# Converting float64 weight blocks one step ahead of their matmuls, in a fused attention and gating kernel

## The chip, the cores and the metric

The kernel runs on one core of a Trainium2 chip. The metric is the device time of one execution in microseconds (us), as the median of several runs.

## The reference

Four batches of 448 tokens go through causal attention with 12 heads, then two mixing layers. Inputs are float64 and the result is float32. Cut to what matters:

```python
attn = softmax_causal(q @ k.T / sqrt(64)) @ v                  # 4 x 12 x 448 x 64
x = attn.transpose(0, 2, 1, 3).reshape(4, 448, 768)
gate = sigmoid(causal_conv5(x, conv_w))                        # 5 taps, each channel alone
x = (gate * (x @ w_val)) @ w_out
theta = x @ w_theta
zr, zi = x * cos(theta), x * sin(theta)
u = x + einsum('ts,bsd->btd', w_tok_r, zr) + einsum('ts,bsd->btd', w_tok_i, zi)
out = u + maximum(u @ w_ch, 0)
```

The four dense weights, w_val, w_out, w_theta and w_ch, are 768 x 768 each.

## The kernel before

The program is written for five engines: TensorE (PE, matmuls), VectorE (DVE), ScalarE (ACT), GpSimd (POOL) and SyncE (SP, which issues the transfers). It interleaves two streams. One is attention, in `attn_iter` (L673), one head in five segments: scores, row maximum by DVE (L360), exp by ACT (L118), transposes of the probabilities (L379), the product with v (L402), and, per pair of heads, the reciprocal of the sums (L418), which goes to DRAM in small packets (`rows<-rec`, L425) and comes back broadcast (`rb<-rows`, L451) to scale the attention's result (`xf`, L462). The other is `dense(b)` (L552): six output blocks each of w_val, w_out, w_theta and w_ch for one batch, all in transposed form with 128 channels per block. While batch b's dense stream runs, the attention of batch b+1 is advanced between its steps by a rate table.

A weight block, numbered n = 0 to 23 for the first batch (0 to 5 w_val, 6 to 11 w_out, 12 to 17 w_theta, 18 to 23 w_ch), holds 768 x 128 weights in two halves g. A half, written here as 16.0 or 16.1, passes through four steps:

- `load_w` (L197 on, issue at L202): SP brings 384 KB of float64 words into a buffer of tag "wb" (8 buffers), named `cv_raw`.
- `stage_w` (L210): `to_f32` (L153) builds float32 bits from the two 32-bit words of each number: DVE at L156 and L159 into a PSUM buffer `ps_cv`, ACT at L162, DVE at L163 back into `cv_raw`.
- `split_w` (L214): the float32 block is split into a high part of fewer bits (POOL, L107) and the rest (POOL, L110, or DVE, L113, in the first halves of w_theta), into a second "wb" buffer `w_hl`. The float32 block (`plain`, L221, w_val and w_out) or the split one (`scratch`, L242, w_theta and w_ch) is stored in DRAM for the later batches.
- In `gemm` (L519), 18 matmuls (L532) for a block: three for each 128 of the 768 inputs, high by high, high by low, low by high.

`gemm(n)` works half by half, and ahead of the matmuls of half g of block n it asks for the later blocks' steps. In the kernel before these are, at L524 to L527, the split of block n+1, the conversion of n+2, the load of n+3 (and for later batches the fetch from DRAM of n+3). Blocks 0 and 1 are multiplied inside the attention of batch 0, and blocks 0 to 3 are converted there (the table `A_TILES`), in the kernel before as in the changed one. From the second batch on no block is converted; blocks come back from DRAM (L250).

In the w_theta part, `theta(e)` makes for each block a tile `z`: t = theta/2pi (L587), rounding (L588, L589), absolute value (L591, on DVE in this batch), sine and cosine on ACT (L600, L601), products with x (L602 on DVE, L603 on POOL). `ztr` (L613) transposes z on PE, `tok` (L627) multiplies by the token weights. ACT needs a table load (ACT_TABLE_LOAD) between exp and sine. In the w_ch part each block ends with L665 on DVE, and transposes (L654) and an output store (L659).

The framework orders each engine's instructions when the program is built, with a model of time and of the data each one needs; on the chip every engine then works strictly in that fixed order, the queue of SP too. So moving one call in `gemm` can shift the place of many instructions.

Of the kernel before, what the change touches and what calls it, by code (L numbers as in the profile page):

```python
# [33 lines left out]
AHEAD = 2  # L34
# [17 lines left out]
def kernel(  # L52
# [46 lines left out]
    def f32(ap):  # L99
        return ap.bitcast(F32)  # L100

    def psum(tag):
        at = "mm" if tag == "mm" else "at"
        return ps.tile([P, 512], F32, tag=at, name=f"ps_{tag}", bufs=2 if tag == "mm" else 6)

    def pool_hi(dst, src):
        nc.gpsimd.tensor_scalar(out=dst, in0=src, scalar1=1.0, scalar2=0.0, op0=ALU.mult, op1=ALU.add)  # L107
# [45 lines left out]
    def to_f32(dst, raw):  # L153
        hi, lo = raw[:, :, 1], raw[:, :, 0]
        low = psum("cv")[: raw.shape[0], : raw.shape[1]].bitcast(I32)
        nc.vector.tensor_scalar(  # L156
            out=low, in0=lo.bitcast(U32), scalar1=2.0**-29, scalar2=7.0, op0=ALU.mult, op1=ALU.min
        )
        nc.vector.scalar_tensor_tensor(  # L159
            out=low, in0=hi, scalar=-(2**31), in1=low, op0=ALU.bitwise_and, op1=ALU.bitwise_or  # L160
        )
        nc.scalar.activation(lo.bitcast(F32), hi.bitcast(F32), AF.Abs, scale=2.0**-112)  # L162
        nc.vector.scalar_tensor_tensor(  # L163
            out=dst.bitcast(I32), in0=lo, scalar=3, in1=low, op0=ALU.logical_shift_left, op1=ALU.bitwise_or
        )
# [28 lines left out]
    def words(t):  # L194
        return t.rearrange("p n two -> p (n two)")[:, 0:CV]

    def load_w(n, g):  # L197
        if n >= NW:
            return
        e = n % KC  # L200
        t = pool.tile([P, CV, 2], I32, tag="wb", name="cv_raw", bufs=8)
        nc.sync.dma_start(  # L202
            out=t.rearrange("p (c n) two -> p c (n two)", c=KH),
            in_=stages[n // KC][g * KH * P : (g + 1) * KH * P, 2 * e * P : 2 * (e + 1) * P].rearrange(
                "(c p) n -> p c n", p=P
            ),
        )
        bits[n, g] = t

    def stage_w(n, g):  # L210
        if n < NW:
            to_f32(words(bits[n, g]), bits[n, g])

    def split_w(n, g):  # L214
        if (n, g) not in bits:
            return
        flat = words(bits.pop((n, g))).bitcast(F32)
        t = flat.rearrange("p (c n) -> p c n", n=P)
        kept = n % NW // KC in PLAIN
        if B > 1 and kept and n < NW:  # L220
            nc.sync.dma_start(out=plain[n, g], in_=flat)  # L221
        store = B > 1 and (kept and B > 2 if n >= NW else not kept)
        if n < AHEAD:
            hi, lo = (
                pool.tile([P, S], F32R, tag=tag, name="w_ahead", bufs=12)[:, : KH * P].rearrange("p (c n) -> p c n", n=P)
                for tag in ("act_hi", "act_lo")
            )
        else:
            hl = pool.tile([P, 2, KH, P], F32R, tag="wb", name="w_hl", bufs=8)
            hi, lo = hl[:, 0], hl[:, 1]  # L230
        if n < NW:
            pool_hi(hi, t)
        else:
            nc.scalar.copy(hi, t)  # L234
        (dve_lo if n < NW and int(W_DVE[n // KC]) > g else pool_lo)(lo, t, hi)
        if store and n < AHEAD:
            for a, x in enumerate((hi, lo)):
                nc.sync.dma_start(
                    out=scratch[n, g][:, a * KH * P : (a + 1) * KH * P], in_=f32(x.rearrange("p c n -> p (c n)"))
                )  # L240
        elif store:
            nc.sync.dma_start(out=scratch[n % NW, g], in_=f32(hl.rearrange("p a c n -> p (a c n)")))  # L242
        splits[n, g] = (hi, lo)

    def fetch_w(n, g):
        if not NW <= n < NW * B:
            return
        if n < 2 * NW and n % NW // KC in PLAIN:
            t = pool.tile([P, CV, 2], I32, tag="wb", name="cv_raw", bufs=8)
            nc.sync.dma_start(out=words(t).bitcast(F32), in_=plain[n % NW, g])  # L250
            bits[n, g] = t
            return
        hl = pool.tile([P, 2, KH, P], F32R, tag="wb", name="w_hl", bufs=8)
        nc.sync.dma_start(out=f32(hl.rearrange("p a c n -> p (a c n)")), in_=scratch[n % NW, g])
        splits[n, g] = (hl[:, 0], hl[:, 1])
# [263 lines left out]
    def gemm(acts):  # L519
        n = wn[0]  # L520
        wn[0] += 1
        pt = psum("mm")
        for g in range(2):
            split_w(n + 1, g)  # L524
            stage_w(n + 2, g)
            load_w(n + 3, g)
            fetch_w(n + 3, g)  # L527
            whi, wlo = splits.pop((n, g))
            for kc in range(g * KH, (g + 1) * KH):
                xhi, xlo = acts[kc]  # L530
                for m, (a, x) in enumerate(((whi, xhi), (whi, xlo), (wlo, xhi))):
                    nc.tensor.matmul(  # L532
                        pt[:, :S], lhsT=a[:, kc % KH, :], rhs=x,
                        start=kc == 0 and m == 0, stop=kc == KC - 1 and m == 2,
                    )
            if g == 0:
                yield
        return pt
# [13 lines left out]
    def dense(b):  # L552
# [8 lines left out]
        for e in range(KC):  # L561
            if b == 0 and e < AHEAD:
                pt = ahead.pop(e)
                if YLD:
                    yield
            else:
                pt = yield from gemm(xs)
            hf = pool.tile([P, S], F32, tag="tmp", name="hf")
            hf_ins.append(
                nc.vector.scalar_tensor_tensor(  # L570
                    out=hf, in0=gates.pop((b, e)), scalar=1.0, in1=pt[:, :S], op0=ALU.add, op1=ALU.mult
                )
            )
            h_hl[e] = hl(hf, dve=H_LO[b])
            yield
        for e in range(KC):
            pt = yield from gemm(h_hl)
            x2f[e] = pool.tile([P, S], F32, tag="x2f", name="x2f", bufs=6)
            nc.scalar.activation(x2f[e], pt[:, :S], AF.Copy, scale=0.5)
            x2_hl[e] = hl(x2f[e], 0.5, pt[:, :S], dve=O_LO[b])  # L580
            yield

        def theta(e):
            pt = yield from gemm(x2_hl)
            z = pool.tile([P, 2, S], F32, tag="z", name="z", bufs=3)
            t, kk = z[:, 1, :], z[:, 0, :]
            nc.scalar.activation(t, pt[:, :S], AF.Copy, scale=INV_2PI)  # L587
            nc.vector.tensor_scalar(out=kk, in0=t, scalar1=ROUND, scalar2=ROUND, op0=ALU.add, op1=ALU.subtract)  # L588
            nc.vector.tensor_tensor(out=t, in0=t, in1=kk, op=ALU.subtract)  # L589
            if ABS_DVE[b]:  # L590
                nc.vector.tensor_scalar(  # L591
                    out=kk.bitcast(I32), in0=t.bitcast(I32), scalar1=0x7FFFFFFF, scalar2=None, op0=ALU.bitwise_and
                )
            else:
                nc.scalar.activation(kk, t, AF.Abs)
            zri[e] = z
            with ExitStack() as st:
                for ins in exps[-PIN:]:
                    st.enter_context(tc.issue_after(ins.ins))
                nc.scalar.activation(t, t, AF.Sin, scale=TWO_PI)  # L600
                nc.scalar.activation(kk, kk, AF.Sin, bias=halfpi, scale=-TWO_PI)  # L601
            nc.vector.tensor_tensor(out=kk, in0=kk, in1=x2f[e], op=ALU.mult)  # L602
            (nc.vector if Z_DVE[b] else nc.gpsimd).tensor_tensor(out=t, in0=t, in1=x2f[e], op=ALU.mult)  # L603
            yield
# [190 lines left out]
```

## Time and profile before

| | us |
|---|---|
| median of 3 runs (lowest, highest) | 778.81 (778.42, 780.77) |
| the profiled execution's own time | 784.47 |
| its span | 782.4 |
| PE busy | 714.7 (91% of the span) |
| DVE busy | 463.3 (59%) |
| ACT busy | 445.0 (57%) |
| POOL busy | 331.9 (42%) |

The span is the time from the first to the last instruction that the profiler saw. The mean granted clock of PE was 0.967 of full speed. The trace gives each instruction's start and length, and for idle time of an engine ahead of an instruction what released it. The dense stream of batch 0, which alone converts blocks in `gemm`, runs from about 100 to 300 us.

### The profile page before, as it was taken

How to read it: one execution, taken by the hardware profiler on the slowest of the kernel's cores; microseconds unless marked ns; L12 is line 12 of the kernel's file. 1: busy time of each engine (PE TensorE's matmuls, PEld its weight loads, DVE VectorE, ACT ScalarE, POOL GpSimd, SP SyncE). 2: the span in 40 equal slices, each digit the busy share in tenths (PEclk: the TensorE clock that was granted, in tenths of full speed). 3: DMA queues.
4: the chain of work that ended last, by engine and by line, in shares of the span. 5: the costliest groups of instructions: out<-in, count | busy, mean ns of one | idle time of the engine just before them, and what ended most of it. 6: DMA issues, size and time to landing. Idle time of an engine off the chain costs nothing.

```text
span 782.4 us, 12216 instructions
## 1 busy us (share of the span) xinstructions
PE 714.7 (91%) x4009; PEld 607.5 (78%) x4009; DVE 463.3 (59%) x1104; ACT 445.0 (57%) x1047; POOL 331.9 (42%) x363
## 2 busy tenths in 40 slices
PE   5898978994988998999899999999899998999997
PEld 4665666783867886888688798898788887898996
DVE  4888599887777564463575564564576432115531
ACT  4787665876797454565877344354878331125401
POOL 0597774975476566774164410033062241201100
PEclk9999889998999999899999999999999999999999
DMA  9845337988684398799843288688532187774223
GB/s 227 181 122 146 78 106 224 208 265 187 193 143 123 103 208 279 233 224 338 152 75 99 54 171 232 193 141 240 143 61 66 52 135 233 203 220 139 84 71 81
DMA packets 152940, 125.78 MB, mean 161 GB/s; under 512 B 92815, under 2 KB 130477, under 8 KB 152877
## 3 DMA queue, kind: packets, MB, share of 16 engines
q1 hardware_dynamic: 152877, 125.00, 62.9%
q8 instruction: 32, 0.52, 0.3%
q14 instruction: 31, 0.25, 0.1%
HBM read 95.81 MB, written 29.16 MB: 160 GB/s over the span
## 4 chain that ended last, share of the span: by engine, by line
PE 58%; DVE 15%; ACT 10%; DMA 9%; issue 4%; POOL 2%; SPq 2%; DVEq 0%; ACTq 0%; POOLq 0%
PE ps_mm L532 31%; PE ps_mm L627 11%; PE ps_av L402 5%; PE ps_tr L379 3%; ACT prob L118 2%; DMA cv_raw<-in_moe_w_theta_dram 2%; PE ps_s L358 2%; PE ps_s L359 2%; DVE qs L113 2%; DMA scratch<-w_hl 2%; DVE ps_s L360 2%; DVE gate L494 2%; DVE klo L113 1%; DMA out_dram<-o 1%; DVE ps_cv L156 1%
## 5 line engine op out<-in xcount | busy, mean ns | idle before, releaser
L532 PE MATMUL ps_mm<-act_hi,w_hl 128*128 128x448 f32 x864 | 267.5, 372 | 1.4 <-DVE w_hl L113 0.7
L532 PEld LDWEIGHTS ps_mm<-act_hi,w_hl 128*128 128x128 f32 x864 | 161.7, 190 | 14.7 <-DVE w_hl L113 1.1
L532 PE MATMUL ps_mm<-act_lo,w_hl 128*128 128x448 f32 x432 | 157.9, 367 | 0.0
L360 DVE CUSTOM_DVE_ANT_0 ps_s<-ps_s,mask 112x112 f32<-112x112 f32 x192 | 85.9, 455 | 66.9 <-PE ps_s L359 53.8
L118 ACT ACTIVATE prob<-ps_s,negm 112x112 f32<-112x112 f32 x192 | 95.2, 497 | 50.6 <-DVE negm L360 49.3
L110 POOL TENSOR_TENSOR act_lo<-x2f,act_hi 128x448 fp32r<-128x448 f32 x36 | 42.8, 1188 | 109.8 <-DVE act_hi L544 52.2
L392 ACT COPY pt<-ps_tr 112x448 f32<-112x448 f32 (+3 forms) x132 | 53.6, 425 | 61.6 <-PE ps_tr L379 61.2
L379 PE MATMUL ps_tr<-ident,prob 112*112 112x112 f32 x480 | 78.4, 271 | 10.6 <-ACT prob L118 4.0
L532 PE MATMUL ps_mm<-x_hi,w_hl 128*128 128x448 f32 x264 | 83.4, 386 | 5.0 <-ACT x_hi L467 2.2
L532 PEld LDWEIGHTS ps_mm<-act_lo,w_hl 128*128 128x128 f32 x432 | 81.7, 190 | 5.0
L358 PE MATMUL ps_s<-kk,qs 128*112 128x256 f32 x192 | 71.7, 377 | 9.4 <-POOL kk L107 3.2
L379 PEld LDWEIGHTS ps_tr<-ident,prob 112*112 112x112 f32 x480 | 56.5, 137 | 24.8 <-ACT prob L118 7.0
L110 POOL TENSOR_TENSOR w_hl<-cv_raw,w_hl 128x384 fp32r<-128x384 f32 x62 | 64.5, 1042 | 13.5 <-ACT w_hl L234 10.9
L627 PE MATMUL ps_mm<-wtok_h,zt_h 128*128 128x448 f32 x168 | 63.8, 380 | 4.3 <-ACT zt_h L618 4.1
L627 PE MATMUL ps_mm<-wtok_h,zt_l 128*128 128x448 f32 x168 | 63.1, 375 | 0.6 <-DVE zt_l L113 0.5
L359 PE MATMUL ps_s<-klo,qs 128*112 128x256 f32 x192 | 62.0, 329 | 1.5 <-DVE klo L113 1.5
L627 PE MATMUL ps_mm<-wtok_l,zt_h 128*128 128x448 f32 x168 | 61.7, 367 | 0.0
L532 PEld LDWEIGHTS ps_mm<-x_hi,w_hl 128*128 128x128 f32 x264 | 51.7, 198 | 12.1 <-ACT x_hi L467 2.9
L603 POOL TENSOR_TENSOR z<-z,x2f 128x448 f32<-128x448 f32 x18 | 20.7, 1148 | 93.5 <-ACT z L600 93.5
L402 PE MATMUL ps_av<-pt,v_raw 112*64 112x448 f32 (+3 forms) x384 | 59.3, 430 | 0.5 <-ACT prob L118 0.5
L490 POOL TENSOR_TENSOR gate<-gate,tp 128x448 f32<-128x448 f32 x48 | 57.5, 1198 | 2.4
L110 POOL TENSOR_TENSOR x_lo<-xf,x_hi 128x448 fp32r<-128x448 f32 x23 | 27.9, 1213 | 61.1 <-ACT x_hi L467 60.5
(108 smaller groups left out, 1352.8 us busy)
## 6 DMA issues: line engine op xcount, KB each, us to landing
w_hl<-scratch SPq DMA_DIRECT2D x120, 384.0 KB, 3.8
scratch<-w_hl SPq DMA_DIRECT2D x48, 384.0 KB, 4.2
q_raw<-in_q_dram SPq DMA_DIRECT2D x48, 112.0 KB, 3.6
v_raw<-in_v_dram SPq DMA_DIRECT2D x24, 224.0 KB, 4.2
out_dram<-o SPq DMA_DIRECT2D x24, 224.0 KB, 3.3
cv_raw<-in_moe_w_val_dram SPq DMA_DIRECT2D x12, 384.0 KB, 5.3
plain<-cv_raw SPq DMA_DIRECT2D x24, 192.0 KB, 3.8
cv_raw<-in_moe_w_out_dram SPq DMA_DIRECT2D x12, 384.0 KB, 4.6
```

What stands on the lines that cost most here:

```text
L110: nc.gpsimd.tensor_tensor(out=dst, in0=src, in1=f32(hi), op=ALU.subtract)
L113: return nc.vector.tensor_tensor(out=dst, in0=src, in1=f32(hi), op=ALU.subtract)
L118: exps.append(nc.scalar.activation(*args, **kw))
L358: nc.tensor.matmul(pt[:CP, :nn], lhsT=qs[:, cs], rhs=kk[:, :nn], start=True, stop=False)
L359: nc.tensor.matmul(pt[:CP, :nn], lhsT=qs[:, cs], rhs=klo[:, :nn], start=False, stop=True)
L360: ttr = nc.vector.tensor_tensor_reduce(out=pt[:CP, :n], in0=pt[:CP, :n], in1=mask[:, S - n : S], scale=-1.0 / math.sqrt(D), scalar=3.0e38, ...
L379: nc.tensor.transpose(pt[:CP, off : off + CP], prob[i, c][:, kc * CP : (kc + 1) * CP], ident[:CP, :CP])
L392: nc.scalar.copy(t, src)
L402: nc.tensor.matmul(av[g][j * D : (j + 1) * D, kc * CP : S], lhsT=tv[:, j, kc, :], rhs=pT.pop((2 * g + j, kc)), start=kc == 0, stop=kc == N ...
L490: nc.gpsimd.tensor_tensor(out=gt, in0=gt, in1=tp, op=ALU.add)
L532: nc.tensor.matmul(pt[:, :S], lhsT=a[:, kc % KH, :], rhs=x, start=kc == 0 and m == 0, stop=kc == KC - 1 and m == 2,)
L627: nc.tensor.matmul(pt[:, :S], lhsT=a[:, m, :], rhs=w[:, m, :], start=m == 0 and n == 0, stop=m == NZ - 1 and n == 2,)
```

## The change

`gemm` calls `stage_w` for block n+1, directly ahead of that block's split, where it called it for n+2 behind the split of n+1. The condition leaves out the blocks that the attention part has converted. So the conversions of blocks 4 to 23 (20 blocks, two halves each) move by one block step; loads, splits and matmuls are asked for in the same steps as before. The file gets one line longer: lines from 526 on count one more in the changed kernel.

```diff
--- before.py
+++ after.py
@@ -521,8 +521,9 @@
         wn[0] += 1
         pt = psum("mm")
         for g in range(2):
+            if n + 1 >= AHEAD + 2:
+                stage_w(n + 1, g)
             split_w(n + 1, g)
-            stage_w(n + 2, g)
             load_w(n + 3, g)
             fetch_w(n + 3, g)
             whi, wlo = splits.pop((n, g))
```

What the built programs' orders show at three places. The names: `cv_raw_2307`, `_2327`, `_2370`, `_2402`, `_2446` are blocks 15.0, 15.1, 16.0, 16.1 and 17.0 in the kernel before; `cv_raw_2297`, `_2317`, `_2360` are 15.0, 15.1 and 16.0 in the changed one.

SP, theta part, before:

```order
L202 DMA cv_raw_2307<-in_moe2_w_theta_dram 128x3x256
L242 DMA scratch_76<-w_hl_2298 128x768
L290 DMA q_raw_2266<-in_q_dram 112x4x64 x2
L202 DMA cv_raw_2327<-in_moe2_w_theta_dram 128x3x256
L290 DMA k_raw_2269<-in_k_dram 112x4x64 x2
L242 DMA scratch_76<-w_hl_2318 128x768
L202 DMA cv_raw_2370<-in_moe2_w_theta_dram 128x3x256
L425 DMA rows_2275<-rec_2272 112x8x1
L242 DMA scratch_76<-w_hl_2361 128x768
L202 DMA cv_raw_2402<-in_moe2_w_theta_dram 128x3x256
```

SP, the same place, changed:

```order
L290 DMA q_raw_2256<-in_q_dram 112x4x64 x2
L242 DMA scratch_76<-w_hl_2203 128x768
L290 DMA k_raw_2259<-in_k_dram 112x4x64 x2
L425 DMA rows_2265<-rec_2262 112x8x1
L202 DMA cv_raw_2297<-in_moe2_w_theta_dram 128x3x256
L242 DMA scratch_76<-w_hl_2293 128x768
L202 DMA cv_raw_2317<-in_moe2_w_theta_dram 128x3x256
L202 DMA cv_raw_2360<-in_moe2_w_theta_dram 128x3x256
L242 DMA scratch_76<-w_hl_2313 128x768
L202 DMA cv_raw_2392<-in_moe2_w_theta_dram 128x3x256
```

The load of 15.0 stood seven rows ahead of `rows<-rec` and now stands right behind it; 16.0 stood right ahead of it and now follows four rows behind.

DVE, theta part, before (`z_2338` is the first z, `z_2413` the second):

```order
L156 TENSOR_SCALAR ps_cv_2397<-cv_raw_2327 128x384
L589 TENSOR_TENSOR z_2338<-z_2338 128x448
L588 TENSOR_SCALAR z_2413<-z_2413 128x448
L156 TENSOR_SCALAR ps_cv_2441<-cv_raw_2370 128x384
L159 SCALAR_TENSOR_TENSOR ps_cv_2397<-cv_raw_2327,ps_cv_2397 128x384
L360 ISA ps_s_2387,negm_2265<-ps_s_2387,mask_67 112x224
L360 ISA negm_2265 112x1
L591 TENSOR_SCALAR z_2338<-z_2338 128x448
L589 TENSOR_TENSOR z_2413<-z_2413 128x448
L360 ISA ps_s_2430,negm_2265<-ps_s_2430,mask_67 112x336
L360 ISA negm_2265 112x1
L159 SCALAR_TENSOR_TENSOR ps_cv_2441<-cv_raw_2370,ps_cv_2441 128x384
```

DVE, the same place, changed (`z_2328` is the first z, `z_2403` the second):

```order
L156 TENSOR_SCALAR ps_cv_2427<-cv_raw_2297 128x384
L360 ISA ps_s_2377,negm_2255<-ps_s_2377,mask_67 112x224
L360 ISA negm_2255 112x1
L163 SCALAR_TENSOR_TENSOR cv_raw_2207<-cv_raw_2207,ps_cv_2383 128x384
L159 SCALAR_TENSOR_TENSOR ps_cv_2427<-cv_raw_2297,ps_cv_2427 128x384
L360 ISA ps_s_2420,negm_2255<-ps_s_2420,mask_67 112x336
L360 ISA negm_2255 112x1
L589 TENSOR_SCALAR z_2328<-z_2328 128x448
L360 ISA ps_s_2447,negm_2255<-ps_s_2447,mask_67 112x448
L360 ISA negm_2255 112x1
L163 SCALAR_TENSOR_TENSOR cv_raw_2297<-cv_raw_2297,ps_cv_2427 128x384
L590 TENSOR_TENSOR z_2328<-z_2328 128x448
```

Ahead of the 224-wide row maximum (the first ISA row) stood the first instruction of 16.0's conversion and now stands that of 15.0's; the absolute value of the first z (L591, now L592) follows three rows behind the last one shown, and 16.0's conversion only behind the products of the third z.

POOL, w_ch part, before (`w_hl_3419`, `_3439`: 21.0 and 21.1; `w_hl_3482`: 22.0):

```order
L107 TENSOR_SCALAR w_hl_3419<-cv_raw_3223 128x384
L110 TENSOR_TENSOR w_hl_3419<-cv_raw_3223,w_hl_3419 128x384
L107 TENSOR_SCALAR w_hl_3439<-cv_raw_3257 128x384
L110 TENSOR_TENSOR w_hl_3439<-cv_raw_3257,w_hl_3439 128x384
L483 TENSOR_SCALAR gate_3406<-xf0_72,cw_68 128x448
L487 TENSOR_SCALAR tp_3407<-xf0_72,cw_68 128x448
L107 TENSOR_SCALAR kk_3375<-kk_3375 64x448
L490 TENSOR_TENSOR gate_3406<-gate_3406,tp_3407 128x448
L110 TENSOR_TENSOR x_lo_3403<-xf0_72,x_hi_3402 128x448
L107 TENSOR_SCALAR w_hl_3482<-cv_raw_3304 128x384
```

POOL, the same place, changed (`w_hl_3414`, `_3434`: 21.0 and 21.1):

```order
L483 TENSOR_SCALAR gate_3396<-xf0_72,cw_68 128x448
L487 TENSOR_SCALAR tp_3397<-xf0_72,cw_68 128x448
L107 TENSOR_SCALAR kk_3365<-kk_3365 64x448
L490 TENSOR_TENSOR gate_3396<-gate_3396,tp_3397 128x448
L110 TENSOR_TENSOR x_lo_3393<-xf0_72,x_hi_3392 128x448
L107 TENSOR_SCALAR w_hl_3414<-cv_raw_3213 128x384
L487 TENSOR_SCALAR tp_3397<-xf0_72,cw_68 128x448
L107 TENSOR_SCALAR w_hl_3434<-cv_raw_3247 128x384
L107 TENSOR_SCALAR kk_3372<-kk_3372 64x448
L110 TENSOR_TENSOR w_hl_3414<-cv_raw_3213,w_hl_3414 128x384
L490 TENSOR_TENSOR gate_3396<-gate_3396,tp_3397 128x448
L110 TENSOR_TENSOR w_hl_3434<-cv_raw_3247,w_hl_3434 128x384
```

The split of block 21 stood ahead of the gate (L483) and x_lo instructions and now stands behind and between them, where 22.0 stood.

## Rows read from the trace of the kernel before

**Rows 1.** Windows: us, busy of PE, PEld, DVE, ACT, POOL, then PEclk, DMA share, GB/s.

```profile
100.00:150.00 50.00, 42.48 (x217) 34.25 (x217) 48.51 (x108) 32.61 (x76) 32.72 (x37) 0.93 0.69 188
150.00:200.00 50.00, 38.49 (x213) 31.58 (x213) 39.34 (x87) 36.43 (x85) 33.47 (x39) 0.86 0.87 220
...
250.00:300.00 50.00, 50.00 (x287) 43.63 (x288) 29.84 (x73) 25.49 (x68) 34.91 (x43) 0.97 0.69 164
300.00:350.00 50.00, 46.36 (x248) 39.90 (x247) 26.13 (x60) 29.30 (x74) 32.08 (x32) 0.93 0.82 240
```

**Rows 2.** Waits of DVE and of PE, 95 to 300 us: total, times, longest.

```profile
DVE ps_cv L156 <- DMA cv_raw<-in_moe_w_theta_dram: 6.2, 6, 3.6
...
PE ps_tr L613 <- DVE z L602: 9.2, 1, 9.2
```

**Rows 3.** Timeline of DVE: start us, us, instruction, idle before it.

```profile
177.87 0.19 DVE L418 RECIPROCAL rec<-rec 112x8 f32<-112x8 f32 x1
...
188.02 0.56 DVE L156 TENSOR_SCALAR ps_cv<-cv_raw 128x384 int32<-128x384 uint32 x1 [3.62 <-DMA cv_raw<-in_moe_w_theta_dram]
...
194.17 0.61 DVE L602 TENSOR_TENSOR z<-z,x2f 128x448 f32<-128x448 f32 x1
```

**Rows 4.** Timeline of PE.

```profile
185.37 0.36 PE L532 MATMUL ps_mm<-act_hi,w_hl 128*128 128x448 f32 x1
194.93 1.73 PE L613 MATMUL ps_tr<-ident,z 128*128 128x128 f32 x7 [9.19 <-DVE z L602]
```

**Rows 5.** Timeline of ACT.

```profile
190.45 1.28 ACT L600 ACT_TABLE_LOAD   x1
```

**Rows 6.** SP's timeline, theta; landing of 16.0 and 16.1, of 11.1, of all cv_raw.

```profile
178.04 0.39 SPq L202 DMA_DIRECT2D cv_raw<-in_moe_w_theta_dram  x1
178.52 0.53 SPq L425 DMA_DIRECT2D rows<-rec  x1
...
DMA to landing us min/median/max: 9.9/10.0/10.0
...
DMA to landing us min/median/max: 8.2/8.5/8.8
...
DMA to landing us min/median/max: 2.6/4.5/10.0
```

**Rows 7.** Tile cv_raw, 100 to 300 us: ns min/median/max, first and last start.

```profile
L156 DVE TENSOR_SCALAR ps_cv<-cv_raw x40: 538/560/598, 105.8 to 283.2; 128x384 int32<-128x384 uint32 x40
L162 ACT ACTIVATE cv_raw<-cv_raw x40: 533/560/607, 106.5 to 283.8; 128x384 f32<-128x384 f32 x40
```

**Rows 8.** Timeline of POOL, w_ch.

```profile
271.67 1.01 POOL L110 TENSOR_TENSOR w_hl<-cv_raw,w_hl 128x384 fp32r<-128x384 f32 x1
...
276.12 0.64 POOL L483 TENSOR_SCALAR gate<-xf,cw 128x448 f32<-128x448 f32 x1 [1.00 <-DVE xf L462]
...
280.34 0.52 POOL L107 TENSOR_SCALAR w_hl<-cv_raw 128x384 fp32r<-128x384 f32 x1
...
282.21 1.02 POOL L110 TENSOR_TENSOR w_hl<-cv_raw,w_hl 128x384 fp32r<-128x384 f32 x1
...
292.35 0.51 POOL L107 TENSOR_SCALAR w_hl<-cv_raw 128x384 fp32r<-128x384 f32 x1 [4.47 <-PE ps_av L402]
```

**Rows 9.** Timeline of PE, w_ch.

```profile
280.45 0.45 PE L532 MATMUL ps_mm<-act_hi,w_hl 128*128 128x448 f32 x1
...
292.27 0.47 PE L532 MATMUL ps_mm<-act_hi,w_hl 128*128 128x448 f32 x1
```

**Rows 10.** SP's timeline, w_ch; landing of the load issued at 279.29.

```profile
276.42 1.38 SPq L290 DMA_DIRECT2D k_raw<-in_k_dram  x2
...
279.29 0.39 SPq L202 DMA_DIRECT2D cv_raw<-in_moe_w_ch_dram  x1
...
280.37 0.44 SPq L425 DMA_DIRECT2D rows<-rec  x1
...
DMA to landing us min/median/max: 3.8/3.8/3.8
```

## The prediction

> **What bounds the kernel now.** I read the windows first, because the change touches one stage only: batch 0's dense chain, about 100 to 300 us of the span. There TensorE (PE) is busy 42.48 and 38.49 us of the first two 50 us, and all 50.00 of 250 to 300 us [rows 1]. So some time can be won before 200 us and none at 250 to 300, where whatever delays PE costs in full. VectorE (DVE), which does the conversions, is the fuller engine in the first stretch: 48.51 of 50 [rows 1]. Then I read the waits of that stage. The longest single wait of PE is 9.2 us, for the z products of the theta part; DVE waits 6.2 us in six pieces for loads of w_theta words, one of them 3.6 us [rows 2].
>
> The timeline joins the two. DVE starts the conversion of block 16.0 (block 16, first half) at 188.02, when its load has landed, 3.62 us late [rows 3]. Behind it in DVE's fixed order stand the row maximum of the 224-wide scores, the absolute value of the first z, and at 194.17 the first z product. ScalarE (ACT) cannot load the sine table before the exp of those scores: 190.45 [rows 5]. PE's last matmul before is at 185.37, its next instruction, z's transposes, at 194.93 [rows 4]. So a conversion whose result PE wants much later holds up PE.
>
> Why was the load late? It was issued at 178.04, and half a microsecond behind it stands `rows<-rec`, a store in small packets [rows 6]. This load and the next, behind the store, took 9.9 and 10.0 us; the median of all cv_raw transfers of the stage is 4.5; a load of block 11 issued 3.5 us behind another `rows<-rec` took 8.2 to 8.8 [rows 6]. Loads just before or behind that store are slow ones.
>
> **The change, part by part.** No conversion is added or removed: 20 blocks in two halves each, of three DVE instructions (about 0.56 us each) and one ACT instruction, keep their work [rows 7]. What changes is where they stand.
>
> *DVE-bound start (100 to 150 us).* At the same place of the attention work one block fewer is converted: 6 x 0.56 = 3.4 us less DVE work ahead of it [rows 7]. That is a lead that is not built, no saved time; the split of a block then comes nearer to its matmuls. I take 0 for PE, with bounds from -1.5 to +1.5 us (half of those 3.4 us either way, since PE idles 7.5 us of this stretch for several reasons [rows 1]). The loads of w_val and w_out blocks stay the same distance ahead of their conversion, since each is issued behind the plain store of a block two steps earlier, and that store moves too.
>
> *Theta.* In DVE's new order the conversion that stands ahead of the 224-wide scores and of z is that of 15.0, and 16.0 follows only behind the z products. The stall of 16.0 goes. But SP now issues 15.0's load right behind `rows<-rec`, where 16.0 and 16.1 were. `rows` waits for the reciprocal, at 177.87 before [rows 3]. With 3.4 us less DVE work in front I put it at 174.6, the load of 15.0 at 175.6; with 9.0 us to landing (between 8.2 and 10.0 [rows 6]) DVE starts it at 184.6. From there to the transposes it was 194.93 - 188.02 = 6.9 us before; after, 12 DVE instructions of about 0.45 us pitch stand between this conversion and z's absolute value, then the cosine, the product and the hand-over, so I take 7.0. PE would go on at 191.6 instead of 194.93: **-3.3 us**. Bounds: with the reciprocal no earlier, the load is issued at 178.9, lands after 9.9 at 188.8 and PE goes on at 195.8 (+0.9); with a landing in the median 4.5 us DVE would be there at 180.1, earlier than it can be done with its other work, so the floor is PE's own last matmul, 185.4, plus some 5 us of z's chain, 190.4 (-4.5).
>
> *ACT.* The new order has the exps of all four score groups before the first sine, and then sine and cosine of two z's together: 2 table loads fewer, 1.28 us each [rows 5]. One stays on the path above; the two that go stand beside it, so I count 0; at most 1.7 us could come.
>
> *w_ch.* PE is never idle here, so this is where the shorter lead is paid. Before, GpSimd (POOL) split block 21.0 by 272.7 (start 271.67) [rows 8], and PE took it at 280.45 [rows 9]: 7.8 us of lead. In the new POOL order the split of 21.0 stands behind the gate and x_lo instructions that begin at 276.12, where 22.0 stood before. Putting the times of 22.0's two instructions there, its hi part starts at 280.34, and its lo part, one more hi of 0.5 us later, at 282.7, ending 283.7 [rows 8]. PE's third matmul of block 21 needs it, at 280.85: 2.9 us late. From there POOL has no gap up to block 23's split; before, it idled 4.47 us ahead of 292.35 [rows 8] while PE was held by nothing [rows 1]. The same durations in POOL's new order let its last split of the stage, 23.1, end near 295.3, and the nine matmuls of that half, at 0.36 us or less each [rows 9], near 298.3, where the second half of block 23 was done by 297.3 before (5 us behind 292.27 [rows 9]): 1.0 us late. Between 2.9 at the stage's middle and 1.0 at its end I take **+2.0**, since PE's attention work there moves too; bounds 0 (the delay is made up in the 3.64 us that PE idles in the next stretch [rows 1]) and +4.7 (below).
>
> *Edits with no cost:* the new `if` runs when the program is built; blocks 0 to 3 are converted in the attention part in both; from the second batch on the order of the engines is the same.
>
> **Sum.** -3.3 + 2.0 + 0 = -1.3 us. The profiled execution took 784.47 us, 5.66 over the median of the runs, 778.81; the sum carried to the median gives **777.5 us**. About 0.3%, 2.3 us, is what a measurement of this kernel can tell from no change.
>
> **The rivals.**
>
> *A larger gain.* 15.0's load escapes the slow landing (6.9 us or less), the z chain runs at its floor (-4.5) and w_ch's delay vanishes in the idle time behind it: 774.3. For it: dense(1) begins with idle PE [rows 1]. Against it: the loads behind a `rows<-rec` took over 8 us, 16.1 and 11.1 among them [rows 6].
>
> *Slower: loads caught by the small-packet store in both places.* In theta 15.0 then lands at 188.8 (+0.9 or 0). In w_ch the load of 23.0, which stood ahead of the q and k loads, now stands behind them, and `rows<-rec` right behind it: issue at 277.8, the end of k's issue [rows 10], landing 9.9 us later, as 16.0 did [rows 6], at 287.7. Against it: 23.1's load, issued 1.1 us ahead of the next `rows<-rec`, took 3.8 us [rows 10]. The last conversion instruction of 22.0 stands behind the first of 23.0 in the new DVE order, so 22.0 is not split before 290.4; POOL's order wanted its hi at 286.3. That delays the rest by 2.7 us, in all +4.7. It decides from a landing of 23.0 later than 285 us on this clock. Price +2.0 to +5.6, as one number +3.5: 782.3. The Trainium skill, "DMA: Bandwidth & Descriptors", section "Rules for kernel authors", says to issue a DMA early and to wait for it late; the change does the opposite of the first half for the w_ch loads, and by that rule this rival is the one to expect. The trace agrees in part: 16.0 was issued 6 us before DVE was free for it and came late all the same [rows 3, 6].
>
> *The change does nothing.* If the planner had put the same rows in another place only on paper, the time would stay 778.8; the order shows that DVE, SP and POOL differ all through the stage, so this has no chance of its own; the time of it lies in the forecast's range.
>
> **How the numbers follow.** Forecast (a smaller stall in theta, a delay in w_ch): 0.45, own range 775.5 to 780.0, most of it within 0.3%. Larger gain: 0.25. Slower: 0.30. From these: faster by over 0.3% is 0.25 and 0.12 of the forecast's chance, 0.37; slower 0.29 of the rival's 0.30; the rest, 0.34, is within. The range takes in the larger gain with the ACT term, 774.3 - 1.7 = 772.6, and the slower rival to nearly its end, 778.8 + 4.7 = 783.5; I leave out what lies beyond, under 2 in 10.
>
> **What would show it.** Right: DVE waits for a w_theta load once, for 15.0, ending near 184.6; PE's wait for the z products is about 6 us and not 9.2; in 275 to 295 us PE has waits for w_hl from POOL of 2 to 3 us; ACT has two table loads fewer. Wrong: no wait on 15.0 (larger gain); a wait of DVE on a w_ch load of several microseconds, with `rows<-rec` next to it (slower); or PE waits for w_hl between 104 and 150 us that were not there before, which would mean that the lead was needed already in the first blocks.

## The result, and the profile after

The change makes the kernel **slower: 1.0054 times the time of the kernel before, 95% interval 1.0029 to 1.0079**, that is +4.2 us on 778.81 (+2.3 to +6.2). The medians of 15 runs each are 787.02 and 783.46 us; their quotient, 1.0045, lies in the same interval. Runs of one and the same kernel lie up to 13 us apart here and the chips differ a little (the kernel before had medians of 780.0 to 783.5 over all comparisons), so only ratios of runs made side by side are compared below. The profiled execution of the changed kernel is one of its quick ones, 784.06 us, nearly that of the kernel before, 784.47; what the two traces differ in is read by places, not by their ends.

The windows of the changed kernel, as in [rows 1] (busy of PE, PEld, DVE, ACT, POOL, then PEclk, DMA share, GB/s):

```profile
100.00:150.00 50.00, 38.98 (x205) 30.84 (x204) 46.35 (x104) 31.45 (x77) 26.69 (x33) 0.86 0.60 160
150.00:200.00 50.00, 39.20 (x194) 31.91 (x195) 35.27 (x79) 30.81 (x75) 32.98 (x38) 0.86 0.82 218
...
250.00:300.00 50.00, 44.42 (x240) 36.25 (x240) 29.08 (x72) 24.98 (x65) 31.96 (x40) 0.91 0.58 158
300.00:350.00 50.00, 48.65 (x280) 42.98 (x279) 27.51 (x61) 28.76 (x71) 33.51 (x33) 1.00 0.89 273
```

PE is busy for 38.98 us of the first stretch where it was for 42.48, and at a lower granted clock (0.86 of full speed against 0.93), so the work that it does there falls by more than these 3.5 us. Between 250 and 300 us it is busy for 44.42 where it had been full. In 150 to 200 us it gains 0.71. The stages in which I had expected a loss of nothing and of 2 us each lost more, and the one with the expected gain hardly gained.

The waits behind this, 95 to 310 us (total, times, longest), of DVE:

```profile
DVE ps_cv L156 <- DMA cv_raw<-in_moe_w_out_dram: 6.0, 2, 3.7
DVE ps_cv L156 <- DMA cv_raw<-in_moe_w_theta_dram: 4.7, 2, 4.4
...
DVE ps_cv L156 <- DMA cv_raw<-in_moe_w_ch_dram: 3.3, 1, 3.3
```

and of PE:

```profile
PE ps_tr L379 <- ACT prob L118: 6.1, 1, 6.1
PE ps_tr L655 <- DVE x2f L666: 4.8, 1, 4.8
PE ps_mm L533 <- POOL w_hl L107: 4.3, 1, 4.3
PE ps_s L358 <- DVE wtok_l L113: 3.5, 1, 3.5
PE ps_mm L533 <- DVE w_hl L113: 2.5, 1, 2.5
```

PE's single wait of 9.2 us [rows 2] is gone, and five of 2.5 to 6.1 us stand in its place, in four parts of the stage. DVE now waits for loads of three weights: 3.7 us at the longest for w_out, 4.4 for w_theta, 3.3 for w_ch.

The theta part. The timeline of DVE (start us, us, instruction, idle before it and its releaser):

```profile
176.10 0.19 DVE L418 RECIPROCAL rec<-rec 112x8 f32<-112x8 f32 x1
...
188.47 0.56 DVE L156 TENSOR_SCALAR ps_cv<-cv_raw 128x384 int32<-128x384 uint32 x1 [4.38 <-DMA cv_raw<-in_moe_w_theta_dram]
```

SP's timeline:

```profile
177.43 0.61 SPq L425 DMA_DIRECT2D rows<-rec  x1
178.14 0.66 SPq L202 DMA_DIRECT2D cv_raw<-in_moe_w_theta_dram  x1
```

The tile cv_raw in the window of that load alone, from issue to landing:

```profile
DMA to landing us min/median/max: 10.2/10.2/10.2
```

PE's timeline:

```profile
190.20 0.47 PE L533 MATMUL ps_mm<-act_hi,w_hl 128*128 128x448 f32 x1 [4.31 <-POOL w_hl L107]
...
193.36 1.11 PE L533 MATMUL ps_mm<-act_hi,w_hl 128*128 128x448 f32 x2 [2.49 <-DVE w_hl L113]
...
198.74 0.93 PE L614 MATMUL ps_tr<-ident,z 128*128 128x128 f32 x7
```

This is the stall that was foretold, on 15.0 behind `rows<-rec`, but it ends at 188.47, where 16.0's ended at 188.02 [rows 3], and PE starts the transposes of z at 198.74, where it had been 194.93 [rows 4]. Ahead of them PE now does the matmuls of block 14, and these waited for their split, 4.31 and 2.49 us. The split itself began only at 189.63 on POOL. The store `scratch<-w_hl` issued at 178.88, 1.5 us behind `rows<-rec`, took 10.6 us, to 189.46: behind `rows<-rec` stores are late as well as loads. That the split waited for the buffer of this store is read from the two times alone and was not tried.

The w_ch part, DVE's timeline:

```profile
288.97 0.56 DVE L156 TENSOR_SCALAR ps_cv<-cv_raw 128x384 int32<-128x384 uint32 x1 [3.32 <-DMA cv_raw<-in_moe_w_ch_dram]
...
290.83 0.61 DVE L666 SCALAR_TENSOR_TENSOR x2f<-ps_mm,x2f 128x448 f32<-128x448 f32 x1
```

SP's timeline:

```profile
278.54 0.31 SPq L425 DMA_DIRECT2D rows<-rec  x1
278.94 0.51 SPq L202 DMA_DIRECT2D cv_raw<-in_moe_w_ch_dram  x1
```

The landing of the second of these, by its window of the tile:

```profile
DMA to landing us min/median/max: 9.9/9.9/9.9
```

PE's timeline:

```profile
291.60 1.07 PE L655 MATMUL ps_tr<-ident,x2f 128*112 128x128 f32 x4 [4.79 <-DVE x2f L666]
```

The load of 23.1, 0.4 us behind `rows<-rec`, took 9.9 us where it had taken 3.8 [rows 10]. Behind its first conversion instruction stands the relu of block 21 (L666, 290.83), and for that PE waited 4.79 us.

### The profile page after: what moved, and what is told of

It reads as the page before. It is cut to its first block, busy times and chain, and to the rows that moved or that the text cites. A ratio compares the mean times of both kernels' runs of the same rounds, so it can differ in the third digit from the quotient of the medians.

```text
span 782.0 us, 12212 instructions
## 1 busy us (share of the span) xinstructions
PE 710.1 (91%) x4009; PEld 603.1 (77%) x4009; DVE 463.4 (59%) x1104; ACT 441.8 (57%) x1045; POOL 330.7 (42%) x363
## 4 chain that ended last, share of the span: by engine, by line
PE 57%; DVE 14%; ACT 11%; DMA 7%; issue 5%; POOL 4%; SPq 1%; DVEq 0%; POOLq 0%; ACTq 0%
PE ps_mm L533 31%; PE ps_mm L628 11%; PE ps_av L402 5%; PE ps_tr L379 3%; ACT prob L118 2%; PE ps_s L358 2%; PE ps_s L359 2%; POOL w_hl L110 2%; DVE qs L113 2%; DVE ps_s L360 2%; DVE gate L494 1%; DMA tok_bits<-in_moe_w_tok_i_dram 1%; PE ps_tr L614 1%; DVE klo L113 1%; ACT L601 1%
## 5 line engine op out<-in xcount | busy, mean ns | idle before, releaser
L533 PE MATMUL ps_mm<-x_hi,w_hl 128*128 128x448 f32 x264 | 80.5, 375 | 2.5 <-DVE hf L571 1.7
L402 PEld LDWEIGHTS ps_av<-pt,v_raw 112*64 112x64 f32 x384 | 28.3, 145 | 32.3 <-issue 17.7
```

Of the source, the lines that this page charges most:

```text
L402: nc.tensor.matmul(av[g][j * D : (j + 1) * D, kc * CP : S], lhsT=tv[:, j, kc, :], rhs=pT.pop((2 * g + j, kc)), start=kc == 0, stop=kc == N ...
L533: nc.tensor.matmul(pt[:, :S], lhsT=a[:, kc % KH, :], rhs=x, start=kc == 0 and m == 0, stop=kc == KC - 1 and m == 2,)
```

## The experiments

All ran against the kernel before on the same chip. "Late" below means that a block is converted in the step of its split, as in the change; the other blocks stay as before. With LO and HI for the first and last late block:

```diff
-            if n + 1 >= AHEAD + 2:
+            if n + 1 >= AHEAD + 2 and LO <= n + 1 <= HI:
                 stage_w(n + 1, g)
             split_w(n + 1, g)
+            if not LO <= n + 2 <= HI:
+                stage_w(n + 2, g)
```

A second edit, called "wide", takes the `rows<-rec` stores of batch 1 away: the reciprocals come to the channels by four transposes on PE per pair of heads, as batch 0 has it. The reads back, `rb<-rows`, go with the stores. They are not what makes loads late: in the kernel before the six loads issued within 1.5 us of one landed after 4.1 to 5.6 us. Nothing is left out of what the kernel computes.

```diff
-        if g < NP:
+        if g < 2 * NP:
```

| late blocks | rows<-rec in 100 to 300 us | ratio to before, 95% | DVE waits over 1 us for cv_raw loads, 140 to 180 us |
|---|---|---|---|
| none | yes | 1 | 1.67, 1.27 |
| 4 to 23 (the change) | yes | 1.0054 (1.0029 to 1.0079) | 3.67, 2.31 |
| 18 to 23 | yes | 1.0004 (0.9972 to 1.0035) | 3.79 |
| 12 to 17 | yes | 0.9970 (0.9943 to 0.9997) | 2.81 |
| 4 to 11 | yes | 1.0092 (1.0058 to 1.0126) | 2.74, 4.75 |
| 4 and 5 | yes | 0.9997 (0.9968 to 1.0027) | 3.25, 1.23 |
| 6 to 11 | yes | 1.0162 (1.0116 to 1.0209) | 5.97, 7.01 |
| 6 to 23 | yes | 1.0113 (1.0068 to 1.0159) | 6.46, 4.01 |
| none | no | 0.9929 (0.9897 to 0.9960) | 1.58, 1.80 |
| 4 to 23 | no | 0.9958 (0.9925 to 0.9990) | 1.51 |
| 6 to 11 | no | 0.9955 (0.9927 to 0.9983) | 1.71 |
| 12 to 17 | no | 0.9833 (0.9783 to 0.9883) | none |

The waits in the last column are those of one trace each. The 3.79 and 2.81 us of the rows 18 to 23 and 12 to 17 are for the load of 11.0, behind `rows<-rec`, though w_out is converted there as in the kernel before: it landed after 10.5 and 9.9 us, and in the kernel before after 9.0. PE waited for a split at most 1.1 and 0.2 us between 145 and 170 us there. With the longer lead such a wait of DVE hardly reaches PE.

**The three weights apart.** LO, HI = 18, 23; then 12, 17; then 4, 11.

> Only the w_ch blocks (18 to 23) are converted one step later. Theory (loads caught by the small-packet store): a load of block 23 is again issued within 3 us of rows<-rec, takes 9 to 10 us, and DVE waits 2 us or more for it with the relu of an earlier block queued behind; PE loses 4 to 8 us in the stage, part of it regained in the idle time of the next: +2 to +4 us against the kernel before. Rival (the lead itself, by the split's place in POOL's order): PE waits 2 to 3 us for w_hl from POOL, no DVE wait for a w_ch load: +1 to +2 us.

> Only the w_theta blocks (12 to 17) are converted one step later. Theory: the 3.6 us stall of DVE on 16.0 becomes one on another block of w_theta whose load is next to rows<-rec; PE's longest wait falls below 9.2 us but a wait for w_hl comes in its place: -2 to +1 us. Rival (the stall goes with the distance): no DVE wait for a w_theta load over 1 us, and -3 to -5 us.

> Only blocks 4 to 11 (w_val, w_out) are converted one step later. Theory: DVE has waits of 2 to 4 us for a tok_bits load near 110 us and for a w_out load issued behind rows<-rec near 145 to 155 us, PE loses 4 to 7 us before 160 us: +2 to +5 us. Rival (this part is neutral, as forecast): within 1.5 us of the kernel before, PE's waits before 160 us as before (about 4 us in all).

The parts add up: 0.04 - 0.30 + 0.92 = +0.66%, with the whole change at +0.54%; the interval of the change holds both. So the loss is that of w_val and w_out, 7.2 us by itself, the part that the prediction had put at zero.

w_ch alone: the wait that the theory named is there, 2.97 us of DVE for a w_ch load and 4.45 us of PE for the relu behind it, and no wait of PE for w_hl there. The time hardly moves all the same. The windows of 275 to 290, 290 to 305 and 305 to 320 us, first of the kernel before, then of this one, show why:

```profile
275.00:290.00 15.00, 15.00 (x90) 12.91 (x89) 12.15 (x30) 8.91 (x23) 11.54 (x16) 1.00 1.03 177
290.00:305.00 15.00, 15.00 (x91) 13.37 (x90) 4.24 (x13) 6.16 (x16) 9.34 (x10) 1.00 1.03 327
305.00:320.00 15.00, 11.36 (x49) 9.17 (x47) 10.23 (x21) 9.43 (x24) 8.58 (x8) 0.77 0.54 147
```

```profile
275.00:290.00 15.00, 9.75 (x55) 7.46 (x53) 11.85 (x30) 7.68 (x21) 11.02 (x15) 0.99 0.64 167
290.00:305.00 15.00, 15.00 (x82) 12.14 (x81) 2.74 (x8) 5.09 (x12) 9.95 (x12) 0.89 0.83 279
305.00:320.00 15.00, 13.63 (x81) 12.10 (x80) 12.44 (x28) 10.17 (x26) 9.69 (x10) 1.00 0.66 183
```

PE is busy 5.25 us less up to 290 us and 2.27 us more in the window behind 305, where it had been idle for another reason. In this trace 3.0 us are left at 320; the runs give an interval of -2.2 to +2.7 us. So the theory was right on the wait and its +2 to +4 us is met at most at its lower end; the rival's +1 to +2 is neither shown nor excluded.

w_theta alone gains 0.30%. Here too a load on either side of `rows<-rec` (173.51 and 176.67, the store at 175.62) takes 10.4 and 11.4 us. But in the order that the planner made, the next conversion stands behind z's product. The timeline of DVE:

```profile
186.46 1.10 DVE L605 TENSOR_TENSOR z<-z,x2f 128x448 f32<-128x448 f32 x1 [0.54 <-ACT z L604]
...
188.56 0.55 DVE L156 TENSOR_SCALAR ps_cv<-cv_raw 128x384 int32<-128x384 uint32 x1
```

and of PE:

```profile
187.62 0.99 PE L616 MATMUL ps_tr<-ident,z 128*128 128x128 f32 x7 [1.52 <-DVE z L605]
```

DVE does not wait for the load, and z's transposes start 7.3 us earlier than before, of which 2.3 us come out at the end. The rival was right on the waits; the size, 2.3 us with an interval of 0.2 to 4.5, lies between the two expectations.

**Whose loss is it within w_val and w_out?** In the changed kernel's trace the longest wait of PE is at block 4, 6.06 us before 115.12. PE waits there for an exp whose row maximum stands in DVE's order behind conversions of block 4 and of token weights, and DVE itself had waited 2.27 us for a load of token weights up to 110.69. So I took the start for the cause, and tried blocks 4 and 5 alone, the change without them, and the change with the token weights asked for later (`TOK_LOAD = (7, 8, 9, 10)` in place of `(3, 5, 7, 9)`).

> Only blocks 4 and 5 are converted one step later, all others as before. Theory now (the lead was needed at the DVE-bound start: block 4's conversion falls behind token-weight conversions and row maxima on a DVE that is busy 97% of the time, and PE waits for the block): most of the 7 us that the run with blocks 4 to 11 lost, so +4 to +7 us against the kernel before, and PE's longest wait before 130 us 4 us or more. Rival (the 7 us come from the w_out loads next to rows<-rec): within 1.5 us of the kernel before.

> The change for blocks 6 to 23 alone; 4 and 5 stay two steps ahead. Theory (the start costs 4 to 7 us, the rest about nothing): 3 to 7 us below the changed kernel, so -3 to +1 us against the kernel before, with PE's waits before 130 us as before (none over 1.5 us). Rival (loads next to rows<-rec cost it): as the changed kernel, +3 to +5 us.

> The changed kernel, with the four loads and conversions of the token weights asked for at steps 7 to 10 of the dense stream in place of 3, 5, 7 and 9, so that fewer of them stand ahead of block 4's conversion. Theory (block 4 waits behind DVE work that is not urgent): block 4's split is ready near 115 us in place of 119, PE's wait of 6 us before 120 us shrinks to under 3 us, 2 to 6 us below the changed kernel, less what the token work costs where it stands now. Rival (the lead alone counts): the wait stays over 5 us and the time at the changed kernel's.

The theory of the start **fell**. With 4 and 5 late PE loses the 6 us at 115 us, as in the change, but not the time. PE's timeline:

```profile
115.08 0.81 PE L379 MATMUL ps_tr<-ident,prob 112*112 112x112 f32 x3 [6.01 <-ACT prob L118]
...
194.96 1.75 PE L616 MATMUL ps_tr<-ident,z 128*128 128x128 f32 x7 [4.47 <-DVE z L605]
```

The wait for z's product, 9.19 us before [rows 4], is 4.47 us here, and z's transposes start at 194.96 against 194.93. PE came 4.7 us later to a point where it had to wait anyway. That holds for 4 and 5 alone: in the whole change PE's wait for z's product is 0.6 us and can take nothing up. But without 4 and 5 the change is not better, it is worse, 1.0113. With the token weights later block 4's wait stays, 5.42 us, now on its split, and the time is the change's, 1.0045 (1.0013 to 1.0078); that run says nothing more.

**The w_out blocks.** What was left were blocks 6 to 11, with loads beside `rows<-rec`. They were made late alone, once with and once without these stores; and in the changed kernel one single store, the one near 142 us, was taken away (`if g < NP or g == 7`).

> Only the w_out blocks (6 to 11) are converted one step later. Theory now (w_out loads next to rows<-rec take 9 us or more from issue, which is longer than the two steps between a block's load and its conversion; the step that used to lie behind the conversion took that up, and is gone): DVE waits 3 us or more for a w_out load between 145 and 175 us, PE waits behind it, +5 to +9 us against the kernel before. Rival (no part costs by itself, the parts' orders only shift at random): within 2.5 us.

> The same, with batch 1's reciprocals brought by PE transposes, so that no rows<-rec store runs in the dense stream of batch 0. Theory: no DVE wait over 2 us for a w_out load, and the time is that of the kernel before with this route (774.5) within 2.5 us. Rival (the lost step costs with normal landings too): still 5 us or more above that.

> The changed kernel, with one single rows<-rec store taken away, the one near 142 us (pair 7 goes by PE transposes); those near 177 and 278 us stay. Theory: DVE's wait for a w_out load near 153 us is gone, those near 188 us and 289 us stay, and the time falls by 3 to 7 us against the changed kernel, to -4 to +1 us against the kernel before. Rival (many stores or the lead): within 2 us of the changed kernel, +2 to +6 us against the kernel before.

Blocks 6 to 11 alone cost 1.62%, 12.7 us, the largest loss of all and more than the +5 to +9 expected. Without the stores the same kernel is at 0.9955, beside 0.9929 of the kernel before on that route: +0.26%, 2 us. So the stores make about 10 of the 12.7 us, and by the three intervals at least 5. The lost lead shows by itself too, as a wait of PE of 3.39 us up to 132.21, ahead of the store that catches the w_out loads, and of 3.34 us without the stores; the kernel before has none there over 1.2 us. How the stores act, the trace with blocks 6 to 11 late and the stores in place shows. SP's timeline:

```profile
144.72 0.43 SPq L425 DMA_DIRECT2D rows<-rec  x1
...
147.14 0.39 SPq L202 DMA_DIRECT2D cv_raw<-in_moe_w_out_dram  x1
...
151.84 7.35 SPq L221 DMA_DIRECT2D plain<-cv_raw  x2
159.29 0.39 SPq L202 DMA_DIRECT2D cv_raw<-in_moe_w_out_dram  x1
```

DVE's timeline:

```profile
157.78 0.56 DVE L156 TENSOR_SCALAR ps_cv<-cv_raw 128x384 int32<-128x384 uint32 x1 [5.97 <-DMA cv_raw<-in_moe_w_out_dram]
158.25 0.54 DVE L163 SCALAR_TENSOR_TENSOR cv_raw<-cv_raw,ps_cv 128x384 int32<-128x384 int32 x1
...
172.68 1.02 DVE L156 TENSOR_SCALAR ps_cv<-cv_raw 128x384 int32<-128x384 uint32 x2 [7.01 <-DMA cv_raw<-in_moe_w_theta_dram]
```

PE's timeline:

```profile
158.85 0.72 PE L358 MATMUL ps_s<-kk,qs 128*112 128x448 f32 x1 [4.55 <-DVE cv_raw L163]
```

The load of 10.0 goes out at 147.14, 2.4 us behind `rows<-rec`, and DVE, which has waited 5.97 us, can begin with it at 157.78, 10.6 us later. PE waits 4.55 us. Behind it in DVE's order stands the last instruction of 9.1's conversion (158.25), for which SP waits with the plain store of 9.1: the row at 151.84 holds two stores, and SP waits 6.6 us in between. Behind that store stands the load of 11.0, which goes out at 159.29 and not before. So the next loads are late too, and DVE waits again, 7.01 us up to 172.68, for the first w_theta block. One slow landing is paid twice. The transfers of the tile cv_raw in 140 to 160 us land as follows (min/median/max), first with the stores:

```profile
DMA to landing us min/median/max: 1.9/4.8/11.7
```

and then without:

```profile
DMA to landing us min/median/max: 2.0/3.8/5.0
```

With the single store near 142 us taken away, the changed kernel is at 1.0025 (0.9993 to 1.0056): 0.29% or 2.3 us below the change. That lies between the theory's 3 to 7 us and the rival's 2, and the two intervals overlap, so this pair decides nothing by its time. Its trace shows the wait gone: DVE's w_out wait of 3.67 us falls to 1.31 and z's transposes start at 192.86, not 198.74; the wait in w_ch stays, 3.76 us, and so does block 4's, 6.02 us.

**No such stores at all.**

> The order of the kernel before, with the sums' reciprocals of batch 1 brought to the channels by transposes on PE, as batch 0 has it, so that no rows<-rec store runs between 100 and 300 us. Theory: cv_raw loads land in 3 to 6 us throughout; DVE's 3.6 us wait for 16.0 and PE's 9.2 us wait are gone, -3 to -8 us less some us for the added copies and transposes. Rival (the loads are late because the DMA engines are full, rows or no rows): loads of 8 to 10 us remain near 145 and 180 us and the time is not lower.

> The changed kernel, with the reciprocals of batch 1 on the same route by PE, so that no rows<-rec store runs between 100 and 300 us. Theory: no DVE wait of over 2 us for a cv_raw load is left, and the difference to the kernel before with that route is within 2 us. Rival (the shorter lead costs by itself): still 3 to 5 us slower than the kernel before with that route, with PE waiting for w_hl.

The kernel before gains 0.71% by it. The change is +0.29%, 2.3 us, above that (0.9958 beside 0.9929; the intervals overlap), between the 2 us of the theory and the 3 to 5 of the rival, so neither is decided. The rival of the kernel before falls: transfers of cv_raw in 140 to 160 us land in 5.5 us at most there, against 9.0 before. Its 9.2 us wait shrinks to 6.25, and not to nothing, which I had expected: most of it remains when no load is late. In the changed kernel PE then has in w_ch what the prediction had described, waits for the split and no DVE wait for a load. PE's timeline:

```profile
281.15 0.68 PE L533 MATMUL ps_mm<-act_hi,w_hl 128*128 128x448 f32 x2 [0.57 <-POOL w_hl L110]
...
286.54 0.68 PE L533 MATMUL ps_mm<-act_hi,w_hl 128*128 128x448 f32 x2 [1.08 <-POOL w_hl L110]
```

and its window:

```profile
275.00:290.00 15.00, 12.43 (x71) 9.68 (x70) 12.53 (x31) 8.75 (x23) 14.67 (x19) 1.00 0.68 208
```

12.43 us of 15 against 15.00 of the kernel before, with the stores and without them: 2.6 us.

**The part that gains, without the stores.** LO, HI = 12, 17 and wide.

> The one part of the change that gained (w_theta blocks 12 to 17 one step later), together with batch 1's reciprocals by PE and no rows<-rec store between 100 and 300 us. If the two gains are of different waits (order on DVE; landing of loads) they add: -6 to -9 us against the kernel before. If both remove the same 9.2 us wait of PE, they do not: -4 to -6 us, about what the reciprocals' route gave alone.

0.9833, about 13 us: **faster than both kernels**, and more than the two gains together (0.30 and 0.71%) and than the 6 to 9 us expected. They don't remove the same thing: the stores' going takes the late landings, the later conversion takes the order on DVE that remained. What makes the surplus over their sum was not tried. PE reaches z's transposes with a wait of 0.83 us, by its timeline:

```profile
188.94 0.99 PE L616 MATMUL ps_tr<-ident,z 128*128 128x128 f32 x7 [0.83 <-DVE z L605]
```

This run also shows what the stores do not explain. Without them the whole change is at 0.9958 and its theta blocks alone at 0.9833, and the two intervals do not overlap: the other fourteen late blocks, 4 to 11 and 18 to 23, cost about 1.25%, 9.8 us. With the stores they cost 0.84% (1.0054 beside 0.9970). So in the whole change, converting these blocks later costs without any late landing too. In the trace of the changed kernel without the stores PE waits twice ahead of z:

```profile
116.10 0.81 PE L379 MATMUL ps_tr<-ident,prob 112*112 112x112 f32 x3 [4.03 <-ACT prob L118]
...
146.01 1.00 PE L379 MATMUL ps_tr<-ident,prob 112*112 112x112 f32 x4 [2.67 <-DVE cv_raw L163]
```

At z it then waits 1.88 us, where it waits 6.01 with only blocks 6 to 11 late on this route: once the theta blocks are late as well, little of z's wait is left to take such losses up. These two waits and the 2.6 us in w_ch add up to 9.3 us, but no run took them apart.

## Why the prediction was wrong

The forecast was 777.5 us, no change that can be told, with 0.29 for slower; it came out slower by 0.54%. By its own steps:

*The bound and the 9.2 us wait.* Right. A conversion that PE wants much later held up z; when only the theta blocks are moved, the wait is 1.52 us. The sentence that a delay between 250 and 300 us costs PE in full did not hold: with w_ch late PE is busy 5.25 us less there and the time is 1.0004.

*The start, "I take 0 for PE".* **This is the step that failed.** The lost lead was rightly called no saved time, and blocks 4 and 5 by themselves cost nothing, though for another reason than the text had: PE loses 6 us and the z wait takes them up. But the sentence that followed, that the loads of w_val and w_out "stay the same distance ahead of their conversion", was taken as a reason for no cost. The distance is about the same, two steps or some 8 us (4.4 to 11.4 us from issue to conversion for w_out in the kernel before, 4.5 to 10.6 in the changed one). For several of these loads it is shorter than the landing beside `rows<-rec`, which the very same text had put at 8.2 to 10.0 us from [rows 6]. (The 8.2 there is the plain store of 147.97; load 11.1 took 8.8.) In the kernel before, one more step between conversion and matmuls took up such a landing: DVE waited 1.67 us, and PE between 145 and 170 us not once for a split. The timeline of DVE there:

```profile
155.72 0.56 DVE L156 TENSOR_SCALAR ps_cv<-cv_raw 128x384 int32<-128x384 uint32 x1 [1.67 <-DMA cv_raw<-in_moe_w_out_dram]
```

The change takes that step, and the plain store ahead of the next load hands the delay on. Measured, where the prediction had 0: +0.92% (7.2 us) for blocks 4 to 11, +1.62% for 6 to 11. For blocks 6 to 11 alone the late landings are shown to make most of it, since without the stores 0.26% is left. For the whole change they are not: there the blocks other than theta cost as much without the stores, so the lost lead has a price of its own, which the prediction also had at nothing. The prediction applied its own row to theta and w_ch and not to w_out, where the block and the store came as near to each other. The Trainium skill, "DMA: Bandwidth & Descriptors", section "Rules for kernel authors", says to issue a transfer early, compute, and wait for it late. In w_out the change moves the wait later but the issue with it, behind the plain store, so no time is won between the two. The trace agrees: with blocks 6 to 11 late, 10.0's load goes out at 147.14 and not at 139.86, and DVE waits 5.97 and 7.01 us.

*Theta, -3.3.* The mechanism was right (the stall moves from 16.0 to 15.0), the term was mis-sized in the whole kernel: the reciprocal came at 176.10, not 174.6 (with the theta blocks alone at 175.41; PE had lost 6.06 and 3.46 us before 155 us); the load went out at 178.14, not 175.6, and took 10.2, not 9.0. The stall ended at 188.47, near the upper bound given, 188.8. By itself the part is worth -0.30%, 2.3 us.

*ACT, two table loads fewer.* Right: 34 in place of 36. They were counted as 0, and no run tells their price.

*w_ch, +2.0.* The size is near by luck. The forecast's own way, PE waiting for the split on POOL, appears without the stores, where PE loses 2.6 us. With them it loses 5.25 us, by the rival's way, though the load caught was 23.1, not 23.0, and the idle time behind gives about half back. What the runs show of it, +0.04%, is too little to tell from nothing.

*The slower rival.* Its mechanism, loads caught by the small store, is in the trace at all three places and decides for blocks 6 to 11 alone, but the place with most of the loss, w_out, was not among the two it named, and it had no price for the lead itself. That its 782.3 is near the measured 783.0 (778.81 times 1.0054) is luck, the sum of other terms.

What stays open: how the loss of the whole change divides between late landings and the shorter lead, and why blocks 6 to 11 alone cost more than blocks 4 to 11 or the whole change. DVE's waits go with the latter (13.0 us, 7.5 and 6.0 in the table). Block 4's delay may shift the loads against the store; that was not tried by itself.

## What to carry to other kernels

A queue that works in order joins unrelated chains: a conversion that waits for a load holds the row maxima, relus and splits behind it, and a store that waits for that conversion holds the next loads. So a lead is to be compared with the slowest landing near it, not the median, and in every stage that it passes through; a lead that seems idle can be what takes up one late transfer. And a loss on the way costs only what is left of it at the next point that waits for something else; a change that removes this wait makes the earlier losses count.

## What the runs showed of the hardware that I had not expected

The store `rows<-rec` moves 3.5 KB, and it takes 8.6 us (median of 18). In all traces together, the 384 KB weight loads issued up to 4 us behind one took 6.4 to 12.0 us (45 loads between 95 and 310 us, median 9.6), and those over 8 us away from any took 3.0 to 7.0 (337 loads, median 4.2). Of 26 issued up to 2.7 us ahead of one, 20 took 3.2 to 6.5 us and six 8.4 to 10.6, among the latter 16.0 [rows 6], while 23.1, 1.1 us ahead, took 3.8 [rows 10]. The median and size of the store stand in the list of DMA issues of the kernel before:

```profile
rows<-rec SPq DMA_DIRECT2D x18, 3.5 KB, 8.6
```

The Trainium skill, "DMA: Bandwidth & Descriptors", section "Queues, rings and completion order", says that SP owns one ring on each of the 16 DMA engines, and that descriptors are consumed there in ring order. The loads behind the store agree with that; the slow loads ahead of it, 16.0 here and one in the run with w_theta late, are not explained by it.

A long wait of PE can also have a price behind it. The seven transposes of z took 1.73 us in the kernel before, behind a wait of 9.19 us [rows 4], and 0.99 us with the theta blocks alone late, behind 1.52 us. PE was idle from 185.7 to 194.9 us there, and the window from 188.1 to 198.1 us has a granted clock of 0.50 of full speed, which is 1.2 of 2.4 GHz:

```profile
188.10:198.10 10.00, 3.17 (x11) 1.89 (x13) 8.26 (x18) 9.14 (x16) 4.03 (x5) 0.50 0.67 213
```

So equal busy times of PE at different PEclk are not equal work.
